# Causal attention with a gated MLP: the eighth pair of heads transposed by VectorE, and a new order of the steps

## The chip, the cores and the metric

The kernel runs on one core of a Trainium2 chip. The metric is the device time of one execution in microseconds (us), the median of several runs; lower is better.

## The reference

The input is q, k and v of 4 batches, 12 heads, 448 positions and 64 values per head. Causal attention gives x of 448 x 768 in every batch, and a gated MLP follows. Its second half v of the hidden values is normalised, mixed along the sequence by w_sg, and multiplies the first half u:

```python
scores = scale * np.matmul(q, k.transpose(0, 1, 3, 2))
scores = np.where(mask, -1000000000.0, scores)
attn = np.exp(scores - np.max(scores, axis=-1, keepdims=True))
attn = attn / (np.sum(attn, axis=-1, keepdims=True) + 1e-09)
x = np.matmul(attn, v)                       # heads side by side: 448 x 768
h = gelu(x @ w_in)                           # tanh form, 768 -> 1024
u, v = h[..., :512], h[..., 512:]
v_s = np.einsum('ts,bsd->btd', w_sg, layernorm(v) * g_ln) + b_sg[None, :, None]
out = x + (u * v_s) @ w_out                  # 512 -> 768
```

## The kernel before

**Attention.** The heads are worked on in pairs: 24 pairs, numbered from 0, six in each batch, so that the eighth pair has number 7 and is the second of the second batch. For one pair, `pair(p)` records these steps.

- SyncE (SP) loads q and k (line 424).
- TensorE (PE) computes the scores into four PSUM banks, in two steps (line 431). There are eight banks in all.
- VectorE (DVE) adds the mask and takes the maxima, eight instructions with the tile `ngm` (line 446).
- ScalarE (ACT) takes ten exponentials into P, with their sums (line 454).
- VectorE inverts the sums (lines 464 to 466), and two small transfers spread them over the partitions as `rb` (lines 471 and 474).
- P is transposed into B, in one of two ways (below).
- TensorE multiplies B by v in four steps (line 522), VectorE scales the result by `rb` (line 549), and GpSimd (POOL) and ScalarE split it into two parts (lines 555 to 560).

**Two ways to transpose P.** `flip = p >= FLIP` chooses. Without it, TensorE transposes P in four steps of four 128x128 blocks (line 496) into the banks tx and ty, and four copies bring these to B, by ScalarE (line 503) or, for one of the four in the first batch, by VectorE (line 501). With it, VectorE transposes P in two instructions of 1024 columns (line 484) into another P buffer, and four transfers on SP's queue bring this to B (line 488); v lies in another order in DRAM for such a pair. Before, FLIP is 8: pairs 0 to 7 go through TensorE, pairs 8 to 23 through VectorE.

**MLP.** `mlp(b)` needs x of all six pairs of a batch. It records the steps v (by token blocks 0 to 3, tile m, line 577), u (four), s (four) and o (six). All matmuls of the MLP have line 577. Each float32 operand is split into two parts, and three matmuls stand for one product. A step of a group holds three matmuls (`CUT = 3`). The last token block of v has 64 rows: its normalised values go to the tile `vn` in line 636 on VectorE, and every s needs it. The weights w_in, w_out and w_sg are split on the chip during the first batch (lines 350 to 374): VectorE shifts them (368, 370), ScalarE rescales (366), GpSimd casts and subtracts (373, 374).

**The order.** Every step is recorded by `od.add` with an engine, a duration that only a planner outside this file used, and the tiles it reads and writes. The steps are then issued in the order of the table `ORDER`, written out by hand or by that planner; the durations have no other effect on the program. All engines take their instructions in this order, each its own. A step that finds its inputs not ready holds up everything behind it on its engine. SP's queue works the same way: a transfer that waits holds up those behind it.

**The head of the program.** Seven dummy matmuls `warm` (steps 5 to 11, line 339) and one dummy exponential (step 3, line 330) are recorded. In the table before, the dummy matmuls stand behind the transposes of pairs 0 and 1, and the dummy exponential stands at place 1003 of 1883, so that the first exponential that ScalarE meets is one of pair 0 (step 96).

Of the kernel before, what the change touches and what calls it, by code (L numbers as in the profile page):

```python
# [12 lines left out]
AF = mybir.ActivationFunctionType  # L13
# [37 lines left out]
FLIP = 8  # L51
# [174 lines left out]
def attention_gated_mlp(ctx: ExitStack, tc: tile.TileContext, qk, vP, w_in, g_ln, w_sgT, b_sg, w_out, out):  # L226
# [100 lines left out]
    od.add("dve", 0.75, consts2, w=["P0", "sm0"])  # L327
    od.add("pool", 2.4, consts3, w=["P", "sm", ("wsg", "pad")])

    od.add("act", 0.2, lambda: nc.scalar.activation(out=pad[:, 0:1], in_=mhalf, func=AF.Exp), ["sm0"], ["table"])  # L330

    def warm():
        w = wz.t.bitcast(BF16)
# [432 lines left out]
```

## Time and profile before

| what | value |
|---|---|
| median of 3 runs | 339.13 us (338.38 to 340.37) |
| the profiled execution's own time | 337.29 us |
| its span | 335.5 us |
| TensorE busy | 324.1 us, 97% of the span |
| VectorE busy | 251.0 us, 75% |
| ScalarE busy | 208.5 us, 62% |
| GpSimd busy | 175.9 us, 52% |

Busy times are unions of an engine's instructions. An engine that is busy for 75% of the span can be the limit of a part of it, so shares are read by stretches. The chain that ended last goes back from the last instruction, at each step to what released it.

### The profile page before, as it was taken

How to read it: one execution, taken by the hardware profiler on the slowest of the kernel's cores; microseconds unless marked ns; L12 is line 12 of the kernel's file. 1: busy time of each engine (PE TensorE's matmuls, PEld its weight loads, DVE VectorE, ACT ScalarE, POOL GpSimd, SP SyncE). 2: the span in 40 equal slices, each digit the busy share in tenths (PEclk: the TensorE clock that was granted, in tenths of full speed). 3: DMA queues.
4: the chain of work that ended last, by engine and by line, in shares of the span. 5: the costliest groups of instructions: out<-in, count | busy, mean ns of one | idle time of the engine just before them, and what ended most of it. 6: DMA issues, size and time to landing. Idle time of an engine off the chain costs nothing.

```text
span 335.5 us, 7568 instructions
## 1 busy us (share of the span) xinstructions
PE 324.1 (97%) x2590; PEld 266.3 (79%) x2591; DVE 251.0 (75%) x762; ACT 208.5 (62%) x674; POOL 175.9 (52%) x225
## 2 busy tenths in 40 slices
PE   5699999999999999999999999999999999999995
PEld 3467678768887987878888978878989987889994
DVE  4899898999999888967977597889788531644613
ACT  1999999999894637666784526486674302355210
POOL 4258766888986964020535942014256824132691
PEclk9899999999999999999999999999999999999999
DMA  7889968595583688638747858739437440010004
GB/s 227 312 247 307 277 218 267 177 288 160 130 265 103 178 215 235 197 98 226 217 127 214 229 150 204 195 95 243 101 104 206 91 159 3 0 55 2 18 36 164
DMA packets 30965, 56.55 MB, mean 169 GB/s; under 512 B 6096, under 2 KB 15056, under 8 KB 30928
## 3 DMA queue, kind: packets, MB, share of 16 engines
q1 hardware_dynamic: 30928, 56.08, 57.5%
q8 instruction: 20, 0.33, 0.4%
q14 instruction: 17, 0.14, 0.1%
HBM read 33.39 MB, written 5.90 MB: 117 GB/s over the span
## 4 chain that ended last, share of the span: by engine, by line
PE 93%; ACT 4%; DMA 1%; DVE 1%; issue 0%; ACTq 0%; DVEq 0%
PE m L577 65%; PE o L522 13%; PE s L431 11%; ACT P L454 3%; PE ty L496 2%; PE tx L496 2%; DMA qk<-in_qk_dram 1%; PE m L339 0%; ACT L454 0%; ACT vn L366 0%; ACT B L503 0%; DVE s L446 0%; DVE res L702 0%; DVE ngm L446 0%; ACTq L454 0%
## 5 line engine op out<-in xcount | busy, mean ns | idle before, releaser
L454 ACT ACTIVATE P<-s,ngm 128x320 f32<-128x320 f32 (+3 forms) x240 | 102.7, 460 | 28.1 <-DVE ngm L446 19.7
L446 DVE CUSTOM_DVE_ANT_0 s<-s,mask 64x64 f32<-64x64 f32 (+3 forms) x192 | 77.6, 435 | 7.5 <-PE s L431 5.8
L577 PE MATMUL m<-win,x 128*128 128x512 f32 (+1 forms) x264 | 65.9, 399 | 0.0
L577 PE MATMUL m<-g,wout 128*128 128x448 f32 x288 | 61.1, 367 | 0.0
L577 PE MATMUL m<-x,win 128*128 128x448 f32 x288 | 61.1, 367 | 0.0
L577 PEld LDWEIGHTS m<-x,win 128*128 128x128 f32 x288 | 53.9, 188 | 5.0
L577 PEld LDWEIGHTS m<-g,wout 128*128 128x128 f32 x288 | 53.9, 188 | 5.0
L577 PEld LDWEIGHTS m<-win,x 128*128 128x128 f32 (+1 forms) x264 | 47.4, 183 | 11.7
L454 ACT ACTIVATION_READ_ACCUMULATOR P<-s,ngm 128x1 f32 (+1 forms) x240 | 55.1, 233 | 0.0
L431 PE MATMUL s<-qk 64*64 64x64 f32 (+5 forms) x768 | 45.2, 371 | 5.0 <-DMA qk<-in_qk_dram 4.4
L431 PEld LDWEIGHTS s<-qk 64*64 64x64 f32 x768 | 30.7, 139 | 21.6 <-issue 8.5
L522 PE MATMUL o<-B,vraw 128*64 128x64 f32 (+4 forms) x672 | 45.0, 291 | 0.0
L522 PEld LDWEIGHTS o<-B,vraw 128*64 128x64 f32 x672 | 32.8, 137 | 12.7 <-issue 4.5
L484 DVE STREAM_TRANSPOSE P<-P 128x1024 f32<-128x1024 f32 x32 | 38.2, 1224 | 0.7 <-DMA B<-P 0.6
L577 PE MATMUL m<-wsg,vn 128*128 128x448 f32 x176 | 38.3, 369 | 0.0
L621 POOL TENSOR_TENSOR mv<-mv,mhalf 128x1 f32<-128x1 f32 (+1 forms) x16 | 10.0, 626 | 49.0 <-DVE mv L619 40.7
L577 PEld LDWEIGHTS m<-wsg,vn 128*128 128x128 f32 x176 | 32.6, 188 | 3.6 <-DVE vn L636 0.4
L558 POOL TENSOR_TENSOR x<-xt,x 128x448 fp32r<-128x448 f32 x24 | 27.5, 1148 | 14.5 <-ACT x L557 14.2
L702 DVE TENSOR_TENSOR res<-m,res 128x448 f32<-128x448 f32 (+1 forms) x25 | 14.8, 603 | 23.2 <-PE m L577 15.2
L586 DVE SCALAR_TENSOR_TENSOR tmp<-tmp,m 128x448 f32<-128x448 f32 (+1 forms) x28 | 17.9, 640 | 16.2 <-ACT tmp L585 16.0
L673 POOL TENSOR_TENSOR tmp<-tmp,g 128x448 f32<-128x448 f32 x16 | 18.3, 1152 | 18.8 <-DVE tmp L669 18.8
L585 ACT ACTIVATE tmp<-m 128x448 f32<-128x448 f32 (+1 forms) x28 | 15.5, 562 | 20.3 <-PE m L577 19.2
(76 smaller groups left out, 410.8 us busy)
## 6 DMA issues: line engine op xcount, KB each, us to landing
B<-P SPq DMA_DIRECT2D x64, 256.0 KB
qk<-in_qk_dram SPq DMA_DIRECT2D x24, 448.0 KB
vn<-in_w_in_dram SPq DMA_DIRECT2D x12, 512.0 KB
vraw<-in_vP_dram SPq DMA_DIRECT2D x24, 256.0 KB
rb<-rd SPq DMA_DIRECT2D x24, 224.0 KB
out_dram<-res SPq DMA_DIRECT2D x9, 448.0 KB
g<-in_w_out_dram SPq DMA_DIRECT2D x16, 192.0 KB
out_dram<-res SPq DMA_DIRECT2D x5, 224.0 KB
```

The costliest lines, as they stand in the source:

```text
L431: nc.tensor.matmul(out=s[z][bk].t[64 * h:64 * h + 64, col:col + n], lhsT=qk_.t[r, 0, q0:q0 + 64], rhs=qk_.t[r, 1, k0:k0 + n], start=True, ...
L446: nc.vector.tensor_tensor_reduce(out=o, in0=i, in1=mk, scale=-0.125, scalar=3e38, op0=ALU.add, op1=ALU.min, accum_out=ngm[ib[z]][c][0:m])
L454: act(n, lambda c=c, m=m, k0=k0, n=n, bk=bk, col=col, off=off, kc=kc, i=i, z=z: nc.scalar.activation(out=P[i][0:m, off:off + n], in_=s[z][ ...
L484: dve(PW, lambda z=z: nc.vector.transpose(A[ia][:, :, :, z, :].rearrange("p g t k -> p t g k"), P[ib[z]]), Pk[z] + [kp], Ak, 1.105)
L496: nc.tensor.transpose(out, P[ib[z]][:, col:col + 128], ident)
L522: nc.tensor.matmul(out=dst(o.t[r]), lhsT=vr.t[:, c, r], rhs=src(z), start=first and n == 0, stop=last and n == len(lst) - 1)
L558: pool_tt(S, lambda: nc.gpsimd.tensor_tensor(out=y.t[:, S + 64:], in0=x.t, in1=f(y.t)[:, 0:S], op=ALU.subtract), [x, y], [(y, 1)])
L577: nc.tensor.matmul(out=ps.t[0:l().shape[1], 0:n], lhsT=l(), rhs=rr(), start=(k == 0), stop=(k == len(mms) - 1))
L585: act(n, lambda: nc.scalar.activation(out=z(), in_=h(), func=AF.Square), [ps], [t])
L586: dve(n, lambda: nc.vector.scalar_tensor_tensor(out=z(), in0=z(), scalar=1.0 / GC, in1=h(), op0=ALU.add, op1=ALU.mult), [ps], [t])
L673: pool_tt(S, lambda z=z, u=u: nc.gpsimd.tensor_tensor(out=z(), in0=z(), in1=u.t, op=ALU.mult), [u], [t])
L702: dve(hi - lo, lambda rr=rr, ps=ps, z=z, lo=lo, hi=hi: nc.vector.tensor_tensor(out=rr.t[:, z, lo:hi], in0=ps.t[:, lo:hi], in1=rr.t[:, z, l ...
```

## The change

- `FLIP` goes from 8 to 7. Pair 7 has its P transposed by VectorE (two instructions of line 484) and moved by four transfers (line 488). Its four TensorE steps of transposes and their four copies by ScalarE go. TensorE has 522 steps in place of 526, ScalarE 428 for 432, VectorE 515 for 513, SP 212 for 208.
- The exponentials read the key "table" that the dummy exponential writes, so a table has to place that one ahead of them. Both are on ScalarE; no wait is added.
- Durations used by the planner are set anew, and some steps are marked as sharing a port (`port`). This has no effect on the program but through the table.
- `ORDER` is new from end to end.

What the two tables say, as far as the prediction speaks of it:

- The dummy exponential is fourth in the new table. Three dummy matmuls stand ahead of the first scores and four between the scores of pair 1 and the second transpose of pair 0.
- VectorE's step of line 636 in batch 0 (the last token block of v). Ahead of it on VectorE stand, in the new table but not in the old, the two transposes of pair 7, the first transpose of pair 10, the scaling of pair 8 (line 549), one shift of line 368 and one of line 370 of w_out. In the old table but not in the new there stand two steps of line 586 (u) and the halving of two constants (lines 395 and 396).
- TensorE's first step that reads the result of that line 636 (an s step). Ahead of it on TensorE stand, in the new table but not in the old, the four steps of pair 8's multiplication by v. In the old table but not in the new there stand the four transposes of pair 7 and one s step of three matmuls.
- By the time that VectorE has taken the maxima of pair 6, 13 steps of line 368 have gone ahead of them in the new table, and 9 in the old.
- The multiplications by v of pairs 6 and 7 stand next to each other in both tables. The two transposes of pair 7 stand on VectorE ahead of the maxima of pair 9.
- The last TensorE step is one of o's last block in the new table (its result is added in two halves and leaves in two transfers of 112 KB) and one of o's fourth block in the old (one addition, one transfer of 224 KB).

```diff
-FLIP = 8
+FLIP = 7
...
-    84, 85, 86, 1, 4, 0, 2, 89, 87, 90, 96, 88, 95, 98, 91, 92, 97, 99, 93, 94, 125, 126, 128, 127, 12, 18, 13, 103,
...
+    2, 1, 0, 3, 4, 5, 6, 7, 84, 85, 87, 125, 89, 88, 95, 90, 96, 86, 93, 91, 94, 92, 97, 12, 98, 126, 127, 8, 100, 13,
...
-    od.add("act", 0.2, lambda: nc.scalar.activation(out=pad[:, 0:1], in_=mhalf, func=AF.Exp), ["sm0"], ["table"])
+    od.add("act", 1.35, lambda: nc.scalar.activation(out=pad[:, 0:1], in_=mhalf, func=AF.Exp), ["sm0"], ["table"])
...
-                    [s[z][bk], ("ngm", i, c), kp, ks] + ([("P", i, k - 1)] if k == 1 else [("P", i, 2)] if k == 4 else []),
+                    [s[z][bk], ("ngm", i, c), kp, ks, "table"] + ([("P", i, k - 1)] if k == 1 else [("P", i, 2)] if k == 4 else []),
...
-        od.add("dve", 0.42, inv, sk + [ks], [("rT", ip)])
+        od.add("dve", 0.573, inv, sk + [ks], [("rT", ip)])
...
-    def gelu2(ps, m, n, dst=None):
+    def gelu2(ps, m, n, dst=None, port=False):
```

## Rows read from the trace of the kernel before

**Rows 1.** The page, parts 1 and 4: busy time, and the last chain by engine.
```profile
PE 324.1 (97%) x2590; PEld 266.3 (79%) x2591; DVE 251.0 (75%) x762; ACT 208.5 (62%) x674; POOL 175.9 (52%) x225
...
PE 93%; ACT 4%; DMA 1%; DVE 1%; issue 0%; ACTq 0%; DVEq 0%
```
**Rows 2.** The chain that ended last in order of time: start, duration, what.
```profile
3.92 1.88 PE s L431 x8
...
7.07 1.28 ACT L454
...
19.46 0.49 ACT B L503
...
21.40 1.24 PE m L339 x5
...
64.73 0.44 PE tx L496 x4
...
126.64 3.68 PE o L522 x64
...
276.38 55.46 PE m L577 x263
```
**Rows 3.** Stretches: length, busy of PE, PEld, DVE, ACT, POOL, clock, DMA share, GB/s.
```profile
5.94:98.46 92.52, 88.67 (x822) 67.60 (x815) 86.50 (x321) 88.12 (x310) 64.98 (x80) 0.98 0.78 242
...
20.00:60.00 40.00, 39.95 (x417) 28.97 (x419) 37.13 (x146) 39.95 (x151) 27.92 (x33) 1.00 0.85 265
60.00:98.46 38.46, 38.46 (x299) 30.81 (x297) 37.10 (x126) 35.26 (x113) 33.18 (x43) 1.00 0.68 200
```
**Rows 4.** VectorE's timeline from 92 to 104 us: start, duration, line, operation.
```profile
93.87 0.15 DVE L395 TENSOR_SCALAR gcol<-gcol 128x4 f32<-128x4 f32 x1
93.94 0.37 DVE L396 TENSOR_SCALAR bB<-bB 128x448 f32<-128x448 f32 x1
...
96.03 1.13 DVE L586 SCALAR_TENSOR_TENSOR tmp<-tmp,m 128x448 f32<-128x448 f32 x2
...
97.77 0.69 DVE L636 TENSOR_TENSOR vn<-tmp,vn 64x512 fp32r<-64x512 f32 x1
```
**Rows 5.** TensorE's weight loads: what they waited for, total us, times, longest.
```profile
PEld m L577 <- DVE vn L636: 0.4, 2, 0.2
```
**Rows 6.** Groups by line with shapes apart, whole run: busy us, mean ns, idle before.
```profile
L484 DVE STREAM_TRANSPOSE P<-P 128x1024 f32<-128x1024 f32 x32 | 38.2, 1224 | 0.7 <-DMA B<-P 0.6
...
L549 DVE TENSOR_TENSOR xt<-o,rb 128x448 f32<-128x448 f32 x24 | 14.6, 615 | 7.7 <-PE o L522 4.0 <-DMA rb<-rd 2.1 <-POOL x L555 0.7
...
L503 ACT ACTIVATE B<-tx 128x512 f32<-128x512 f32 x16 | 10.0, 703 | 0.0
```
**Rows 7.** Stretches of 1 and of 5 us, columns as in rows 3.
```profile
15.00:16.00 1.00, 1.00 (x17) 0.99 (x11) 0.96 (x5) 1.00 (x7) 0.00 (x0) 0.50 0.15 57
...
65.00:70.00 5.00, 5.00 (x46) 4.03 (x48) 5.00 (x17) 4.97 (x21) 4.40 (x10) 1.00 0.99 262
```
**Rows 8.** Timeline: VectorE's first maximum, ScalarE's first exponential.
```profile
5.94 0.23 DVE L446 CUSTOM_DVE_ANT_0 s<-s,mask 64x64 f32<-64x64 f32 x1 [3.88 <-PE s L431]
...
8.37 0.63 ACT L454 ACTIVATE P<-s,ngm 128x448 f32<-128x448 f32 x1
```
**Rows 9.** TensorE's first scores from 4.6 us, and the same later, from 23 us.
```profile
L431 PE MATMUL s<-qk 64*64 64x448 f32 x4 | 1.8, 978 | 3.9 <-DMA qk<-in_qk_dram 3.9
...
L431 PE MATMUL s<-qk 64*64 64x448 f32 x4 | 1.0, 562 | 0.0
```
**Rows 10.** TensorE's timeline from 92 to 104 us: the s steps.
```profile
94.88 6.18 PE L577 MATMUL m<-wsg,vn 128*128 128x448 f32 x28
```
**Rows 11.** VectorE's groups from 60.00 to 98.46 us: the shifts of w_out.
```profile
L370 DVE SCALAR_TENSOR_TENSOR g<-g 128x192 int32<-128x192 int32 x10 | 3.1, 342 | 0.0
L368 DVE TENSOR_SCALAR g<-g 128x192 int32<-128x192 int32 x9 | 2.9, 337 | 0.0
```
**Rows 12.** VectorE's longest wait from 60.00 to 98.46 us: total, times, longest.
```profile
DVE tmp L586 <- ACT tmp L585: 0.7, 1, 0.7
```

More of the change, by code (lines that the diff above doesn't have):

```diff
@@ L474, in pair @@
         dma(lambda: nc.sync.dma_start(out=rb.t, in_=bass.AP(
-            tensor=rd[ip].tensor, offset=rd[ip].offset, ap=[[512, 8], [0, 16], [1, S]])), [("rd", ip)], [rb], 320e3, dur=0.56)
+            tensor=rd[ip].tensor, offset=rd[ip].offset, ap=[[512, 8], [0, 16], [1, S]])), [("rd", ip)], [rb], 360e3, dur=0.56)
         Pk = [[("P", i, c) for c in range(5)] for i in ib]
@@ L586, in gelu2 @@
         dve(n, lambda: nc.vector.scalar_tensor_tensor(out=z(), in0=z(), scalar=1.0 / GC, in1=h(), op0=ALU.add,
-                                                      op1=ALU.mult), [ps], [t])
+                                                      op1=ALU.mult), [ps], [t], port=port)
         act(n, lambda: nc.scalar.activation(out=z(), in_=z(), func=AF.Tanh, scale=GS * GC), [], [t], True)
@@ L590, in gelu2 @@
         dve(n, lambda: nc.vector.scalar_tensor_tensor(out=z() if dst is None else d.t, in0=z(), scalar=1.0, in1=h(),
-                                                      op0=ALU.add, op1=ALU.mult), [ps, t], [d])
+                                                      op0=ALU.add, op1=ALU.mult), [ps, t], [d], port=port)
         return t, z
@@ L614, in mlp @@
                                                                      op=ALU.add), [ps], [hs])
-                t, z = gelu2(hs, m, DH)
+                t, z = gelu2(hs, m, DH, port=True)
             st, mv = buf(two, "st", [128, 6]), buf(two, "mv", [128, 3])
@@ L622, in mlp @@
                 out=mv.t[0:m, 1:2], in0=mv.t[0:m, 1:2], in1=mhalf[0:m], op=ALU.pow), ["sm0"], [mv])
-            od.add("dve", 0.07, lambda mv=mv, m=m: nc.vector.tensor_scalar(
+            od.add("dve", 0.125, lambda mv=mv, m=m: nc.vector.tensor_scalar(
                 out=mv.t[0:m, 2:3], in0=mv.t[0:m, 0:1], scalar1=mv.t[0:m, 1:2], scalar2=-1.0, op0=ALU.mult, op1=ALU.mult),
@@ L626, in mlp @@
             act(DH, lambda mv=mv, z=z, m=m: nc.scalar.activation(
-                out=z(), in_=z(), func=AF.Identity, scale=mv.t[0:m, 1:2], bias=mv.t[0:m, 2:3]), [mv], [t], True)
+                out=z(), in_=z(), func=AF.Identity, scale=mv.t[0:m, 1:2], bias=mv.t[0:m, 2:3]), [mv], [t], True, 2)
             if m == 128:
@@ L636, in mlp @@
                 dve(DH, lambda y=y, z=z: nc.vector.tensor_tensor(out=y.t[64:128], in0=z(), in1=f(y.t)[0:64],
-                                                                 op=ALU.subtract), [t, y], [(y, 1)])
+                                                                 op=ALU.subtract), [t, y], [(y, 1)], port=True)
             vn[tcn] = y
```

178 rows, old and new, of the table ORDER are left out of this document.

## The prediction

> **What bounds the kernel now.** I began with the page. TensorE is busy for 97% of the span and the last chain is 93% TensorE [rows 1], so the first reading is "bound by TensorE". The chain in order of time says when this is true. ScalarE carries it from 7.07 us, where a load of its function table stands (1.28 us), to the copy that ends at 19.95; from there TensorE carries it without a break worth naming to 276.38 + 55.46 = 331.84 [rows 2]. So there are two lengths to look at: a head in which TensorE waits for ScalarE, and some 312 us in which every microsecond of TensorE counts.
>
> The view by stretches adds what the chain cannot show, who stands close behind. From 20 to 60 us ScalarE is busy 39.95 of 40 us. VectorE is busy 37.13 of 40 there and 37.10 of 38.46 from 60 to 98.46 us [rows 3]. Neither has room there; after the first batch both have. The change takes work from TensorE and ScalarE and gives VectorE more, in just these stretches. The point at which this is decided can be seen: line 636 on VectorE, the last input of the mixing along the sequence, ends at 97.77 + 0.69 = 98.46 us [rows 4], and TensorE waited there, twice for 0.2 us [rows 5]. VectorE and TensorE arrive there together today.
>
> **The change, part by part.**
>
> *TensorE loses the transposes of pair 7:* four steps of 0.44 = 1.76 us, all on the chain, of which the first at 64.73 stands in [rows 2] and the others at 67.26, 67.69 and 68.13 are alike. The multiplication by v takes 3.68 us for two pairs that come through VectorE, or 1.84 for one [rows 2]; the columns multiplied are the same, so I count nothing for it beyond 0.03. Net -1.73 us.
>
> *ScalarE loses four copies,* 4 x 0.70 = 2.8 us at most [rows 6], beside other work. They are worth something only where ScalarE is last.
>
> *VectorE gets two transposes,* 2 x 1.22 = 2.45 us [rows 6]. Behind them in its queue stand the maxima of pair 9, and behind those the exponentials.
>
> *SP gets four transfers* of 256 KB in its queue; the first of them waits for VectorE's transposes, with loads of weights behind it. The DMA engines moved 262 GB/s at a share of 0.99 between 65 and 70 us [rows 7], so 1 MB is some 4 us of them (an estimate from that row). I take nothing: pair 7 is multiplied next to pair 6, as before, several microseconds after its transposes. If that cover fails, the multiplication is late by up to those 4 us; the low end is zero, since nothing becomes earlier.
>
> *The table load moves out of the head.* It ends at 7.07 + 1.28 = 8.35 [rows 2], and the first exponential starts at 8.37 [rows 8]. With the dummy exponential fourth, the load runs while ScalarE has no inputs, and the exponentials start 1.28 us earlier.
>
> *The seven dummy matmuls leave the chain,* where they take about 1.5 us (1.24 for the last five [rows 2]). In the new table they stand where TensorE waits. But ScalarE is full until 60 us, and TensorE cannot run ahead of the copies and exponentials it needs; so I count ScalarE's 1.28 us as TensorE's lead and not the sum of 2.8. Both ends stay for a rival.
>
> *TensorE's clock in the head.* The first 64x448 score matmuls took 978 ns, later ones 562 [rows 9]: the first step ran slowly, and dummies ahead of it may change that by up to 0.9 us, half of the 1.88 that the chain has for it [rows 2]. They may also be too few. Later in the head the granted clock was 0.50, the 1.2 GHz level, between 15 and 16 us [rows 7]; the chain is on ScalarE there, so it cost nothing. I take zero of 0 to 0.9.
>
> *The order.* What counts is what stands ahead of the meeting point at line 636.
>
> For TensorE: out go pair 7's transposes (1.76) and one s step, three matmuls of 6.18/28 = 0.22 [rows 10], 0.66; in comes pair 8's multiplication, 1.84. That is -0.58, and -1.28 for the head: its own arrival goes from 98.46 to 96.6. Behind the point, 331.84 - 98.46 = 233.38 us remain today, and -1.73 + 0.58 = -1.15 of the saving falls here: 232.23.
>
> For VectorE: in come three transposes (3 x 1.22 = 3.67), a scaling (0.61) [rows 6] and two shifts (0.34 + 0.34) [rows 11]; out go two steps of line 586 (1.13) and the halving (0.15 + 0.37) [rows 4]. That is 4.96 - 1.65 = +3.3 us. Against this stands its idle time: from 5.94 us, its first maximum [rows 8], to 98.46 it was busy 86.50 of 92.52, so 6.0 idle [rows 3]. About 1.1 of this are gaps between instructions that stay (from 60 to 98 us it was idle for 1.36 beside 37.10 of work, and 0.9 of this were waits, the longest 0.7 [rows 12]; the other 0.46 make 1.2% of the work); 4.9 were waits. The new table has 13 shifts in place of 9 ahead of pair 6's last maxima, so more work is at hand where VectorE waited. I let it win back 3.5 of the 4.9: an in-order queue always keeps some waits, and from 60 us on, with work at hand, it still had those 0.9. Ends: 0 and 4.9.
>
> **The sum.** VectorE's line 636 ends at 98.46 + 3.3 - 3.5 = 98.26, later than TensorE's 96.6; so it decides, and most of TensorE's lead from the head is lost in waiting here. 98.26 + 232.23 = 330.49 in place of 331.84, **-1.35 us**. The tail (now a smaller last transfer) I leave unchanged. The profiled execution would go from 337.29 to 335.9; it lay 1.84 under the median of the runs shown, so against that median, 339.13 - 1.35 = **337.8 us**, -0.4%. What a measurement of this kernel can tell from no change is about 0.5%, 1.7 us: my forecast lies inside.
>
> **The rivals.**
>
> *A. VectorE fills all its waits* (4.9 us). Then line 636 ends at 96.86 and the gain is 98.46 - 96.86 + 1.15 = 2.75: 336.4 us. If the dummies also speed up the first scores, VectorE starts up to 0.9 earlier and TensorE's own arrival goes with it: 3.65, 335.5. For it: the head, where ScalarE starts earlier, and the shifts moved forward. Against it: in-order waits never vanish. With TensorE alone as the limit (the 1.5 us of the dummies too) it would be 4.6, but VectorE cannot be so early.
>
> *B. Slower: VectorE becomes the limit.* It meets as many waits as before on its new path, wins nothing back, and line 636 ends at 98.46 + 3.3 = 101.8; TensorE stands still there for 3.3 us more and ends at 334.0, +2.15: 341.3 us. The tip-over lies at 2.15 us won back. For it: VectorE is at 93 to 96% already, and the transposes of pair 7 push the maxima of pair 9 back. Against it: its waits today are waits for others that will be earlier. The Trainium skill ("VectorE: DVE Perf Modes", Rules for kernel authors) says to transpose 128x128 on TensorE where PSUM will do as destination. By that rule this change goes the wrong way, and rival B is its price here; [rows 2, 6] show that VectorE's 2.45 us for a pair are more than TensorE's 1.76, so the change can pay only where VectorE has idle time.
>
> *C. Nothing to be seen for another reason:* the transfers of pair 7 are late, TensorE waits up to 4 us at its multiplication, and that wait takes the place of the one at line 636: 337.8 to 339.5.
>
> **How the numbers follow.** My forecast, with 2.1 to 4.4 us won back, has 0.55: of this 0.40 lies within 0.5%, and 0.15 (over 3.8 won back) is faster by more. A has 0.27, nearly all of it faster. B has 0.13. C has 0.05, within. Together: faster 0.42, same 0.45, slower 0.13. The range reaches into A down to 335.2, just below its lower price, and into B up to 340.3, where VectorE wins back 1 us; what is left out is B's upper half and luck beyond A, under 2 in 10.
>
> **What would show it.** Right: the table load ahead of 5 us and the first exponential at its maximum's end, near 7.1; no dummy matmul on the chain; transposes of line 496 for 28 steps, not 32; VectorE over 96% busy from 20 to 98 us; and a wait of TensorE for VectorE of 1 to 2 us near line 636 of the first batch, where now it is 0.2. Wrong: if TensorE waits for nothing there and the gain is over 3 us, VectorE had more to win back than I gave it (A). If TensorE waits there for 3 us or more, B. If the wait is at a multiplication by v near 70 to 75 us, C. If ScalarE's first exponential is not earlier, the head was misread.

## The result: 0.7% slower, and VectorE's shifts grew by eight to ten microseconds

The median after is 341.11 us (339.61 to 343.52, 13 runs) against 338.75 (337.71 to 340.37, 13 runs) on the same chip: ratio 1.0073, 95% interval 1.0045 to 1.0100. That is 2.4 us slower, above the range of the prediction. The profiled execution took 343.52 us, the longest of the 13; a second one of the same kernel (below, a_again) has a span of 339.0 in place of 341.7 us, and where the two differ, both are given.

**The page after**, the lines that answer to [rows 1]:

```profile
PE 326.2 (95%) x2587; PEld 264.4 (77%) x2587; DVE 261.1 (76%) x764; ACT 206.9 (61%) x670; POOL 175.2 (51%) x225
...
PE 74%; DVE 15%; DMA 5%; issue 2%; ACT 1%; POOL 1%; DVEq 0%; SPq 0%
```

VectorE holds 15% of the last chain where it held 1% (13% in the second execution), and its busy time grew by 10 us (7.7 in the second), although it got only two instructions more.

**Stretches after**, with the columns of [rows 3]; the first runs from VectorE's first maximum to the end of its line 636, as 5.94 to 98.46 us did before:

```profile
6.02:106.17 100.15, 90.68 (x845) 65.95 (x837) 97.37 (x323) 85.93 (x311) 65.09 (x82) 1.00 0.78 237
20.00:60.00 40.00, 37.22 (x393) 26.24 (x394) 37.57 (x142) 37.64 (x147) 27.28 (x33) 1.00 0.83 258
60.00:98.46 38.46, 34.44 (x259) 26.41 (x258) 38.28 (x94) 28.17 (x91) 27.42 (x35) 1.00 0.72 205
```

From 60 to 98.46 us VectorE is busy for 38.28 of 38.46, and with 94 instructions; before there were 126 in 37.10 us [rows 3]. An engine that does fewer instructions in more time does longer ones, or its instructions have become longer. Groups by line with shapes apart tell which. **The shifts of the weights up to 98.46 us, before:**

```profile
L370 DVE SCALAR_TENSOR_TENSOR vn<-vn 128x512 int32<-128x512 int32 x12 | 8.3, 690 | 0.6 <-ACT vn L366 0.5
L370 DVE SCALAR_TENSOR_TENSOR g<-g 128x192 int32<-128x192 int32 x14 | 5.5, 414 | 0.0
L368 DVE TENSOR_SCALAR vn<-vn 128x512 int32<-128x512 int32 x12 | 5.1, 425 | 0.1
L368 DVE TENSOR_SCALAR g<-g 128x192 int32<-128x192 int32 x15 | 4.4, 319 | 0.0
```

**and after:**

```profile
L370 DVE SCALAR_TENSOR_TENSOR vn<-vn 128x512 int32<-128x512 int32 x12 | 9.4, 783 | 0.4 <-ACT vn L366 0.4
L370 DVE SCALAR_TENSOR_TENSOR g<-g 128x192 int32<-128x192 int32 x11 | 8.9, 813 | 0.0
L368 DVE TENSOR_SCALAR g<-g 128x192 int32<-128x192 int32 x15 | 7.4, 500 | 0.0
L368 DVE TENSOR_SCALAR vn<-vn 128x512 int32<-128x512 int32 x12 | 7.0, 584 | 0.0
```

The same work on the same shapes: 32.7 us for 50 instructions after, 23.3 for 53 before. At the mean lengths of before the 50 would take 12 x 0.690 + 11 x 0.414 + 15 x 0.319 + 12 x 0.425 = 22.7 us, so the shifts are **10.0 us longer** (by the same sum 8.2 in the second execution). Nearly all else of VectorE kept its length (line 484 has 1225 ns on the page after, 1224 in [rows 6]; an exception is line 636 itself, 0.95 us for 0.69).

What a long shift stands beside is in the timelines. **VectorE after:**

```profile
66.10 2.36 DVE L370 SCALAR_TENSOR_TENSOR g<-g 128x192 int32<-128x192 int32 x1
68.38 0.84 DVE L370 SCALAR_TENSOR_TENSOR vn<-vn 128x512 int32<-128x512 int32 x1
69.14 2.15 DVE L370 SCALAR_TENSOR_TENSOR g<-g 128x192 int32<-128x192 int32 x2
...
105.22 0.95 DVE L636 TENSOR_TENSOR vn<-tmp,vn 64x512 fp32r<-64x512 f32 x1
```

**and GpSimd after:**

```profile
65.38 1.16 POOL L353 TENSOR_TENSOR wsg<-tmp,wsg 64x448 fp32r<-64x448 f32 x1 [2.01 <-ACT wsg L352]
66.50 0.63 POOL L373 CAST win<-vn 128x512 fp32r<-128x512 f32 x1
67.09 1.15 POOL L353 TENSOR_TENSOR wsg<-tmp,wsg 128x448 fp32r<-128x448 f32 x1
68.19 0.47 POOL L373 CAST wout<-g 128x192 fp32r<-128x192 f32 x1
68.75 0.94 POOL L374 TENSOR_TENSOR wout<-g,wout 128x192 fp32r<-128x192 f32 x1
69.65 1.43 POOL L374 TENSOR_TENSOR win<-vn,win 128x512 fp32r<-128x512 f32 x1
```

The shift at 66.10 is in flight for 2.36 us while GpSimd runs three instructions back to back, and it ends soon after the third. Beside no GpSimd instruction such a shift takes 0.34 us in both traces, one of w_in 0.69; those of line 368 take 0.25 and 0.42. Counted in the traces up to the end of line 636 (overlaps of more than 0.02 us), 28 of 53 shifts stood beside no GpSimd instruction before, 18 beside nothing but casts or line 621 (which works on one column), and 7 beside one of GpSimd's wider instructions with two inputs (lines 353, 374, 558 and others). After, it is 19, 7 and 29 of 55. In both orders the first two kinds keep those lengths to within 0.2 us. The 29 grew by 12.3 us together, 22 of them by more than 0.1 us each (10.5 us and 20 in the second execution); the 7 of before grew by 1.7 us.

**TensorE after: what it waited for up to 110 us** (total, times, longest), and the end of the chain:

```profile
PE s L431 <- DVE tmp L590: 2.7, 2, 1.6
PE m L339 <- DVE tmp L334: 2.1, 1, 2.1
PE s L431 <- DVE B L501: 1.4, 2, 1.2
PE ty L496 <- ACT P L454: 1.3, 3, 0.8
PE m L577 <- DVE tmp L590: 1.1, 1, 1.1
PE tx L496 <- ACT P L454: 1.1, 1, 1.1
...
```
```profile
282.63 55.56 PE m L577 x263
```

The wait of line 339 is that of the dummy matmuls, ahead of the first scores. Behind it TensorE stands still for VectorE at several places ahead of line 636, for 2.7 + 1.4 + 1.1 = 5.2 us in these rows (1.6 + 1.4 + 0.5 = 3.5 in the second execution). That line ends at 105.22 + 0.95 = 106.17 us, and TensorE at 282.63 + 55.56 = 338.19, which is 232.0 us later.

**The head after**, ScalarE's timeline:

```profile
0.73 1.28 ACT L330 ACT_TABLE_LOAD   x1 [0.73 <-PEq L755]
...
7.17 0.63 ACT L454 ACTIVATE P<-s,ngm 128x448 f32<-128x448 f32 x1 [4.94 <-DVE ngm L446]
```

The table load has left the head, and the first exponential starts at 7.17 in place of 8.37 us [rows 8]. The first scores take 1.93 us on the chain, as before (1.88 in [rows 2]).

### The profile page after: what moved, and what is told of

The parts are those of the page before. It is cut to its first block, busy times and chain, and to the rows that moved or that the text cites. A ratio compares the mean times of both kernels' runs of the same rounds, so it can differ in the third digit from the quotient of the medians.

```text
span 341.7 us, 7550 instructions
## 1 busy us (share of the span) xinstructions
PE 326.2 (95%) x2587; PEld 264.4 (77%) x2587; DVE 261.1 (76%) x764; ACT 206.9 (61%) x670; POOL 175.2 (51%) x225
## 4 chain that ended last, share of the span: by engine, by line
PE 74%; DVE 15%; DMA 5%; issue 2%; ACT 1%; POOL 1%; DVEq 0%; SPq 0%
PE m L577 58%; PE o L522 9%; PE s L431 7%; DVE s L446 5%; DMA rb<-rd 2%; DVE g L370 2%; DVE g L368 1%; DVE P L484 1%; ACT P L454 1%; DVE ngm L446 1%; DMA vn<-in_w_in_dram 1%; DMA rd<-rT 1%; DMA qk<-in_qk_dram 1%; DVE vn L368 1%; DVE vn L370 1%
## 5 line engine op out<-in xcount | busy, mean ns | idle before, releaser
L454 ACT ACTIVATE P<-s,ngm 64x64 f32<-64x64 f32 (+3 forms) x240 | 100.6, 434 | 31.4 <-DVE ngm L446 27.8
L446 DVE CUSTOM_DVE_ANT_0 s<-s,mask 64x64 f32<-64x64 f32 (+3 forms) x192 | 76.6, 436 | 6.7 <-PE s L431 6.0
L577 PE MATMUL m<-win,x 128*128 128x512 f32 (+1 forms) x264 | 65.0, 398 | 1.5 <-DVE tmp L590 1.1
L577 PE MATMUL m<-x,win 128*128 128x448 f32 x288 | 62.2, 368 | 0.2 <-DVE xt L549 0.2
L431 PE MATMUL s<-qk 64*64 64x64 f32 (+5 forms) x768 | 47.2, 364 | 5.4 <-DVE tmp L590 2.7
L454 ACT ACTIVATION_READ_ACCUMULATOR P<-s,ngm 128x1 f32 (+1 forms) x240 | 49.8, 208 | 0.0
L484 DVE STREAM_TRANSPOSE P<-P 128x1024 f32<-128x1024 f32 x34 | 41.1, 1225 | 3.1 <-ACT P L454 2.4
L522 PEld LDWEIGHTS o<-B,vraw 128*64 128x64 f32 x684 | 33.6, 137 | 12.6 <-issue 4.1
L577 PEld LDWEIGHTS m<-wsg,vn 128*128 128x128 f32 x176 | 32.7, 188 | 3.2 <-DVE vn L636 0.4
L689 POOL TENSOR_TENSOR res<-x 128x448 f32<-128x448 f32 x24 | 27.3, 1152 | 7.4 <-DMA out_dram<-res 5.5
L588 ACT ACTIVATE tmp<-tmp 128x448 f32<-128x448 f32 (+2 forms) x32 | 19.1, 602 | 18.1 <-DVE tmp L586 17.9
```

What stands on the lines that cost most here:

```text
L431: nc.tensor.matmul(out=s[z][bk].t[64 * h:64 * h + 64, col:col + n], lhsT=qk_.t[r, 0, q0:q0 + 64], rhs=qk_.t[r, 1, k0:k0 + n], start=True, ...
L446: nc.vector.tensor_tensor_reduce(out=o, in0=i, in1=mk, scale=-0.125, scalar=3e38, op0=ALU.add, op1=ALU.min, accum_out=ngm[ib[z]][c][0:m])
L454: act(n, lambda c=c, m=m, k0=k0, n=n, bk=bk, col=col, off=off, kc=kc, i=i, z=z: nc.scalar.activation(out=P[i][0:m, off:off + n], in_=s[z][ ...
L484: dve(PW, lambda z=z: nc.vector.transpose(A[ia][:, :, :, z, :].rearrange("p g t k -> p t g k"), P[ib[z]]), Pk[z] + [kp], Ak, 1.105)
L522: nc.tensor.matmul(out=dst(o.t[r]), lhsT=vr.t[:, c, r], rhs=src(z), start=first and n == 0, stop=last and n == len(lst) - 1)
L577: nc.tensor.matmul(out=ps.t[0:l().shape[1], 0:n], lhsT=l(), rhs=rr(), start=(k == 0), stop=(k == len(mms) - 1))
```

## Theories and experiments

**Theory S:** the new order puts VectorE's shifts beside GpSimd's splits of the weights; there they are held up, and VectorE becomes the limit up to some 95 us. **Its rivals:** the way that pair 7 now takes costs the time (F), or the new order costs it by waits that have nothing to do with the shifts' length (O). In the short diffs below, numbers are steps of the table `ORDER`; those of a_ kernels are steps of the new table, those of b_ kernels of the old. Each time is a median, with runs of the kernel before on the same chip beside it; the ratios are to these, and times of different chips are best compared by them.

**a_again.** The kernel after, unchanged.

> The changed kernel once more, for a second profile. In the first profile the four groups of VectorE's shifts (lines 368 and 370) took 35.3 us together, against 24.6 before, with the same 56 instructions. Theory S (VectorE's shifts are held up by GpSimd's splits wherever the new table puts the two side by side): 30 us or more again, time 341 +- 1 us. Theory F (the two transposes of pair 7, 2.45 us, are the whole loss, and the long shifts were an accident of one execution): 24 to 28 us, with the time still 341.

341.08 us, ratio 1.0074 [1.0045, 1.0103]. The shifts take 33.5 us over the whole run (24.6 in the kernel before), and line 636 ends at 102.49 + 0.96 = 103.45 us. The loss and the long shifts stand in both executions.

**a_noflip.** The new table, pair 7 through TensorE.

```diff
-FLIP = 7
+FLIP = 8
 ORDER: steps 688, 689 (two transposes) -> 688 to 691 (TensorE's four), 692 to 695 (the copies)
```

> The new table with pair 7 back on TensorE: its four transposes and copies stand where VectorE's two transposes stood. Theory F: the loss goes, 338.8 us or less. Theory S / O: the loss stays, 340 to 343 us, and the shifts take 30 us or more.

343.89 us, ratio 1.0146 [1.0104, 1.0188]; shifts 34.9 us. The time is a little above the range of S and O. Taking the flip back makes the kernel 2.8 us slower than a_again, so F falls: in the new table the flip is a gain, and the loss lies in the table.

**b_flip.** The old table with the flip, the transposes right behind pair 7's last exponential, the transfers behind its small transfer of line 471.

```diff
-FLIP = 8
+FLIP = 7
 ORDER: ... last exponential of pair 7, +688, +689 ... 686, +690, +691, +692, +693 ...
```

> The old table with pair 7 transposed by VectorE: its two transposes stand behind the last exponential of pair 7, its four transfers behind the small transfer of its sums; nothing else moves. Theory F: VectorE is full, so the kernel loses about what the new one lost, 340 to 341.5 us. Theory S / O (it is the new table that loses): TensorE's 1.73 us against VectorE's 2.45 nearly cancel, 337.5 to 339.5 us, and the shifts take 24 to 28 us.

344.82 us, ratio 1.0180 [1.0138, 1.0222], with shifts of 25.0 us: slower than either range that was expected. So the old table loses by the flip, and for another reason than the new one. SP's queue, when each transfer was issued and for how long:

```profile
66.62 0.57 SPq L471 DMA_DIRECT2D rd<-rT  x1
67.28 3.32 SPq L488 DMA_DIRECT2D B<-P  x4
70.65 1.34 SPq L474 DMA_DIRECT2D rb<-rd  x1
```

The reciprocals come behind the two transposes, and the broadcasts and the weights behind the four transfers: the row of line 474 that stood at 62.59 us in the trace before now starts at 70.65. (Some 2.4 of these 8 us were lost before 57 us, where VectorE's line 464 already stood at 56.83 in place of 54.38.)

**b_flip2.** The same, with the transposes behind the reciprocals, and the transfers behind the broadcasts and a load of w_in (steps 646, 687 and 72, which stand further forward in the table).

```diff
 ORDER: ... 685, 686, +688, +689 ... 646, 72, 687, +690, +691, +692, +693, first transpose of pair 8 ...
```

> The old order with pair 7 through VectorE, as in b_flip, but VectorE's two transposes behind the row of reciprocals of pair 7 (line 466) in place of ahead of it, and SP's four transfers behind the two broadcasts (line 474) and the load of w_in in place of ahead of them. Theory F (b_flip lost by SP's queue: it stood still for the transposes with the broadcasts and weights behind it): most of the 6 us goes, 338 to 341 us. If the flip costs the old order because VectorE has no room for 2.45 us more before 98 us: 341 to 344 us, with VectorE over 98% busy from 60 to 98 us.

342.79 us, ratio 1.0130 [1.0093, 1.0166]. A good quarter of b_flip's loss goes, not most of it; where the rest comes from stays open. Its profiled execution was 4 us longer than its median, so the rows tell the place and not the size of the loss. TensorE's longest wait, and VectorE at that time:

```profile
PE o L522 <- DMA vn<-in_w_in_dram: 4.0, 1, 4.0
```
```profile
78.10 1.25 DVE L484 STREAM_TRANSPOSE P<-P 128x1024 f32<-128x1024 f32 x1 [3.12 <-DMA B<-P]
```

The multiplication by v waits 4.0 us for a transfer; the row names a load of w_in, which lies just ahead of pair 7's four transfers in the queue, and VectorE waits for those four by name. This would be the price that rival C had for late transfers, in the old table; but the wait is as long as what this execution took above the median, and b_flip's profile has none like it, so it isn't shown for the usual execution. VectorE was busy for 33.97 of 38.46 us from 60 us on, so the mechanism of the expectation's other branch is not what happened, although the time falls into it.

**a_memset and b_memset.** In both kernels line 374 writes zeros; the low halves of w_in and w_out are left out.

```diff
-pool_tt(n, lambda: nc.gpsimd.tensor_tensor(out=dst(1), in0=f(lo()), in1=f(dst(0)), op=ALU.subtract),
+pool_tt(n, lambda: nc.gpsimd.memset(f(dst(1)), 0.0),
```

> The kernel after, with line 374 (GpSimd's subtraction that makes the low halves of w_in and w_out) replaced by a GpSimd memset of the same 512 or 192 columns to zero; it leaves out the low halves of these weights. GpSimd then reads nothing from SBUF there and is done sooner; the columns that TensorE multiplies are the same. Theory S (VectorE's shifts of lines 368 and 370 are held up by GpSimd's split working beside them): the shifts fall from 33.5 to 35.3 us to at most 28, VectorE's load from 60 to 98 us falls below 37, and the time falls by 3 us or more against the kernel after, to 338 or less. Theory O (the new order loses by waits that have nothing to do with the shifts' lengths): the shifts may fall, but the time stays within 1 us of 341.

> The kernel before with the same memset in place of line 374 (the low halves of w_in and w_out left out), as the baseline for the same edit in the kernel after. Theory S: its shifts were hardly held up (24.6 us), so they stay at 22 to 25 us and the time stays within 1 us of 338.8; the two kernels with the memset differ by less than 1 us. Theory O: the same here, but the kernel after with the memset stays 2 us or more above this one.

After: 338.06 us, ratio 0.9997 [0.9968, 1.0026], 3.0 us under a_again (2.6 by the ratios). Before: 339.70, ratio 1.0034 [1.0012, 1.0055], 1.4 us over its own kernel, a little more than expected; its shifts took 26.3 us, above the 22 to 25 that were expected, and what else it lost by was not followed. With GpSimd's subtraction out of both, the kernel after is 1.6 us faster than the kernel before, where O wanted it 2 us slower and S the two within 1 us. The shifts of the kernel after with the memset, up to 98.46 us:

```profile
L370 DVE SCALAR_TENSOR_TENSOR vn<-vn 128x512 int32<-128x512 int32 x12 | 9.9, 826 | 0.3 <-ACT vn L366 0.3
L368 DVE TENSOR_SCALAR vn<-vn 128x512 int32<-128x512 int32 x12 | 7.1, 589 | 0.0
L370 DVE SCALAR_TENSOR_TENSOR g<-g 128x192 int32<-128x192 int32 x15 | 6.4, 429 | 0.0
L368 DVE TENSOR_SCALAR g<-g 128x192 int32<-128x192 int32 x16 | 5.2, 333 | 0.0
```

Those of w_out fell from means of 813 and 500 ns to 429 and 333; those of w_in stayed long (826, 589); GpSimd's other subtractions (lines 353 and 558) still run beside some of them. The sum of 28.6 us missed the expected 28, and VectorE's load from 60 to 98.46 us, 38.04 us, did not fall below 37. In this kernel GpSimd is also done sooner, so this run alone doesn't say whether the lengths or GpSimd's earlier end gave the time; the next one does.

**a_apart.** The kernel after with every instruction kept; the nine rows with the longest shifts (ten instructions) are moved to where GpSimd was idle.

```diff
 ORDER (step L368 or L370 -> its new place)
 376, 50 -> ahead of 382;  353 -> ahead of 44;  371, 359, 401 -> behind 62;  365, 377 -> ahead of 68
 69 -> behind 68;  418 -> ahead of 424;  GpSimd's 366, 367, 378, 379 -> ahead of 384
```

> The kernel after with the same instructions; in its order table nine of VectorE's shifts (lines 368 and 370, those that ran longest over their length at rest beside a GpSimd instruction) are moved to places where GpSimd stood idle in the trace of the kernel after, and four of GpSimd's splits (lines 373, 374) go behind two of them. Theory S (shifts are held up by GpSimd's instructions): these nine ran some 8.5 us over their length; half or more of it goes, the shifts up to 98 us fall from 33.5 to 35.3 us to below 30, VectorE's line 636 of batch 0 ends 2 us or more earlier than at 105.2, and the time falls by 2 to 4 us against the kernel after, to 337 to 339. Theory O (the new order loses by other waits): 340.5 to 342, whatever the shifts do.

337.65 us, ratio 0.9976 [0.9952, 1.0000], **3.4 us faster than the kernel after** (3.3 by the ratios) from a move of 14 of 1881 steps. The shifts up to 98.46 us take 28.4 us for 55 instructions, and line 636 ends at 99.20 + 0.96 = 100.16 us, 3.3 to 6.0 us earlier than in the two executions of the kernel after. The stretch from VectorE's first maximum to that end, which holds as many of VectorE's instructions (323) as in the kernel after:

```profile
6.03:100.16 94.13, 89.31 (x845) 65.57 (x837) 91.59 (x323) 85.74 (x311) 64.05 (x82) 1.00 0.82 254
```

VectorE is busy there for 91.59 us, against 97.37 and 95.60 in the two executions of the kernel after, and idle for 94.13 - 91.59 = 2.54, against 2.78 and 1.80. So line 636 is earlier because VectorE's instructions are shorter, and not because of other waits. Theory S holds, O falls.

**a_apart2.** Seven more shifts moved.

```diff
 ORDER: 412, 418, 424, 406, 407, 395, 80 -> ahead of 81 (behind line 613)
```

> The kernel with the shifts moved apart (a_apart) once more: six shifts of w_out and one of w_in, which still ran some 2.8 us over their length between 81 and 88 us, go behind line 613, where GpSimd stood idle from 88.1 to 89.6 us. Theory S: their stretching goes as before (the shifts up to 98 us fall from 28.3 to 26 us or less). The time can fall by no more than TensorE still stands idle for VectorE, so 336.4 to 337.6. If VectorE no longer limits there: no change, 337.7.

337.80 us, ratio 0.9974 [0.9960, 0.9989]. The shifts (up to 98.46 us), the stretches from 60 us and from the first maximum to the end of line 636, and VectorE's longest wait for ScalarE:

```profile
L370 DVE SCALAR_TENSOR_TENSOR vn<-vn 128x512 int32<-128x512 int32 x12 | 8.4, 699 | 0.7 <-ACT vn L366 0.5
L368 DVE TENSOR_SCALAR vn<-vn 128x512 int32<-128x512 int32 x12 | 6.0, 503 | 0.0
L370 DVE SCALAR_TENSOR_TENSOR g<-g 128x192 int32<-128x192 int32 x15 | 5.2, 365 | 0.0
L368 DVE TENSOR_SCALAR g<-g 128x192 int32<-128x192 int32 x16 | 4.1, 270 | 0.0
```
```profile
6.08:100.68 94.60, 89.81 (x845) 65.85 (x837) 87.67 (x323) 85.49 (x311) 64.12 (x82) 1.00 0.81 251
60.00:98.46 38.46, 37.04 (x272) 28.87 (x271) 33.78 (x111) 30.97 (x101) 29.04 (x42) 1.00 0.75 225
```
```profile
DVE tmp L613 <- ACT tmp L611: 3.4, 1, 3.4
```

23.7 us for 55 shifts, as short as in the old table, and the time doesn't move: with 33.78 us in 38.46 VectorE is no longer the limit. It waits 3.4 us at line 613 for ScalarE's line 611, which ends at 87.39 us, as in a_apart (87.35), so line 636 ends no earlier (100.68 us). Of the two branches that were expected it is the second.

**b_table, b_dummy, b_head.** The old table with the new head in parts: the dummy exponential alone, the dummy matmuls alone, both.

```diff
 b_table: step 3 -> ahead of 0
 b_dummy: 1, 4, 5, 6, 7 -> ahead of 85;  8, 9, 10, 11 -> ahead of 127
 b_head:  1, 3, 4, 5, 6, 7 -> ahead of 85;  8, 9, 10, 11 -> ahead of 127
```

> The kernel before with the dummy exponential alone moved to the front (the table load out of the head); the dummy matmuls stay where they were. If the 1.6 us that b_head won are ScalarE's 1.28 us handed through to TensorE: 337.2 to 337.8. If they come from the dummy matmuls (1.5 us off TensorE's chain): 338.3 to 338.8.

> The kernel before with the dummy matmuls alone moved as in b_head (three more ahead of the first scores, four ahead of pair 1's second step of scores); the load of the function table stays in the head. If b_head's 1.6 us come from the matmuls alone: 336.8 to 337.4. If the matmuls and the load are worth something only together, since each alone leaves the other engine as the limit of the head: 338 to 339.

> The old table with the head of the new one alone: the dummy exponential second on ScalarE's side ahead of all others, three dummy matmuls ahead of the first scores, four between the two score steps of pair 1. If ScalarE's 1.28 us reach the end: 337.5 us (-1.3). If VectorE at line 636 (98.5 us) takes it back: 338.7 us, with a longer wait of TensorE there. If the dummies too are gained: 336 us. First exponential at 7.1 us in any case.

b_table: 338.56 us, 1.0003 [0.9981, 1.0025]. b_dummy: 337.97, 0.9987 [0.9963, 1.0011]. b_head: 337.18, 0.9955 [0.9925, 0.9985]. Either part alone can't be told from nothing; together they gave 1.6 us in the median. The intervals of the three overlap, so that the two parts are worth more together than alone isn't shown. In the profiled executions they differ in the granted clock (the third number from the end). Stretches of 1 us from 14 us on, first b_table:

```profile
14.00:15.00 1.00, 1.00 (x18) 0.86 (x12) 1.00 (x4) 1.00 (x7) 0.00 (x0) 0.50 0.72 265
15.00:16.00 1.00, 1.00 (x8) 1.00 (x6) 0.94 (x5) 1.00 (x5) 0.80 (x2) 0.50 0.69 168
```

then b_dummy:

```profile
14.00:15.00 1.00, 0.85 (x7) 0.84 (x11) 0.80 (x5) 1.00 (x6) 0.10 (x1) 0.50 0.80 305
15.00:16.00 1.00, 1.00 (x19) 0.98 (x11) 0.97 (x5) 1.00 (x7) 0.00 (x0) 0.50 0.36 131
```

then b_head:

```profile
14.00:15.00 1.00, 0.95 (x20) 0.65 (x10) 0.97 (x4) 1.00 (x7) 0.00 (x0) 1.00 0.70 270
15.00:16.00 1.00, 0.64 (x4) 0.40 (x4) 0.96 (x6) 1.00 (x5) 0.70 (x2) 1.00 0.48 130
```

In these executions TensorE falls to 0.50, the 1.2 GHz level, around 15 us with one part alone and is busy nearly all the time; with both it stays at 1.00 and has time to spare. What in its earlier work makes the difference these rows don't settle: from 12 to 13 us it was busy for 0.69 us in b_table and 0.58 in b_head, both at 1.00. Nor does the clock explain the times. Of b_table's 12 executions 7 have a granted clock of 0.998 or more over the whole span, and their median is 339.07 us, against 337.79 for the other 5. In b_head it is 7 at 336.61 us and 5 at 337.99, in b_head2 7 at 337.96 and 5 at 337.51. Of the 98 executions of the kernel before that ran beside these experiments, 8 have 0.998 or more, with a median of 338.5 us, and the other 90 have 338.7.

**b_head2.** b_head again, beside a_apart2.

> The kernel with the new head alone (b_head, unchanged) on the same chip as the one with the shifts moved apart, to see which is the better of the two: 337.2 as before.

337.66 us, ratio 0.9980 [0.9959, 1.0002]. The two runs of b_head give 1.2 and 1.6 us in the median; the interval of this one just reaches 1. Between it and the kernels with the shifts apart no difference can be told. All of them lie 0.2 to 0.5% under the kernel before, of which only b_head's first run and a_apart2 are wholly clear of it, and some 3 us or more under the kernel after.

## Why the prediction was wrong

**The step that failed is the sum for VectorE, "+3.3 us", in which two shifts came in at "0.34 + 0.34" and all others at the length that they had.** Up to the end of line 636 VectorE worked 97.37 us where it had worked 86.50 [rows 3]: +10.9 us (95.60 in the second execution, +9.1). The groups of its shifts take 34.6 us there for 55 (32.8 in the second execution), where they took 23.3 for 53: 11.3 us more (9.5), of which the sum had 0.68. (An engine's instructions overlap a little at their ends, so the groups add up to somewhat more than its busy time.) I took their length from [rows 11]. There 16 of the 19 stand beside a GpSimd instruction, but all of these beside casts or line 621 and only one of them beside a subtraction too, and I carried this into an order in which 29 of 55 stand beside GpSimd's wider instructions with two inputs. The old trace had the warning: a shift of line 370 took 1.31 us at 58.20, beside a subtraction of line 353 that ran from 57.65 for 1.65 us. I looked at the mean of a stretch that begins at 60.00 us, 342 ns, and this one lies just ahead of it.

**What VectorE wins back came out near in size, and that is luck.** It had 6.0 us of idle time, I let it win back 3.5, and it has 100.15 - 97.37 = 2.78 left, so it won back 3.2 (in the second execution 1.80 are left, 4.2 won back). But that more work at hand fills its waits isn't shown: in a_apart2, with the shifts back at their old length, VectorE idles for 94.60 - 87.67 = 6.93 us, and wins back nothing. That waits shrink on an engine that is itself late would fit both. Nor is it a proof of the sum that a_apart2's 337.80 us meets the forecast of 337.8: there VectorE's work grew by 1.2 us and not by 3.3. And "busy" on an engine that is held up in the middle of an instruction is no work: "VectorE over 96% busy" came true ((37.57 + 38.28) / 78.46 = 97%) for the wrong reason.

**The meeting point.** Line 636 should have ended at 98.26 and ended at 106.17, in the second execution at 103.45. From there I gave TensorE 232.23 us; it took 232.0 in both. So the parts of the sum that belong to TensorE (pair 7's transposes, pair 8's multiplication moved) stood to 0.2 us, and the whole error lies ahead of this point. The wait of 1 to 2 us "near line 636" didn't come: there it is 0.4 us, and TensorE's waits for VectorE stand earlier, at scores and at v.

**Rival B** gave 341.3 us, and 341.11 was measured. It was right in that VectorE becomes the limit; its price is not what happened, so the agreement is luck: it let VectorE win nothing back for +3.3 us of work, and there were 3.2 to 4.2 us less of idle time for +9.1 to +10.9 us of work. The rule of the Trainium skill that stood beside B ("VectorE: DVE Perf Modes", Rules for kernel authors: transposes on TensorE) is not borne out in the new table: with pair 7 back on TensorE the kernel is 2.8 us slower (a_noflip). In the old table it is: there the way through VectorE costs 4.5 to 6.0 us (b_flip2, b_flip).

**Rival C** is not seen in the kernel after, where none of TensorE's listed waits up to 110 us is for a transfer of pair 7. "I take nothing" for SP's four transfers held. In the old table one execution of b_flip2 shows such a wait (4.0 us), with the reserve given there.

**The head** came as foretold in its times (7.17 for 7.1 us, no dummy matmul on the chain). Zero for the first scores held (1.93 us for 1.88, with three dummy matmuls ahead). The clock I counted as costing nothing, since "the chain is on ScalarE there"; the executions of b_table and of the kernel before that kept it were not faster, so no cost of it is shown. The sum for the head, 1.28 us of TensorE's lead, lies between the medians of the two runs of b_head (1.2 and 1.6), whose intervals are wider than that.

**Why the mechanism could have been known.** That shifts become long beside GpSimd is shown by the two moves (a_apart, a_apart2), which change nothing but the order. The Trainium skill names a cause ("SBUF — State Buffer", Who interferes with whom): a VectorE instruction with two SBUF inputs contends with a GpSimd instruction that reads SBUF, but not with one that only writes it, and one of the two waits for the other. This agrees with line 370, whose shifts have two inputs: in a_memset one kept its 0.68 us beside a memset (from 29.12 us), which took its usual 0.51, and the shifts of w_out fell. It says nothing of line 368, whose shifts have one input and made 5.7 of the 12.3 us (5.7 of 10.5 in the second execution); in b_memset one of them took 1.36 us at 87.36, beside a cast and memsets. In these traces the loss went with the number of meetings with GpSimd's wider two-input instructions, 7 and 29 by the count above; I did not look for them in the old trace.

## What to carry to other kernels

A duration read from a trace belongs to its neighbours too. Before a step is costed at its mean, look at the longest of its group, over the whole run, and at what the other engines did just then; where there is a long one, a new order must be costed by how often it brings the two together. And an edit that gains in one order can lose in another (the flip: 2.8 us gained in the new table, 4.5 to 6.0 lost in the old), so test it in the order that it comes with.

## What was not expected of the hardware

- A VectorE instruction in flight was overtaken by several of GpSimd's. The shift at 66.10 us was in flight when GpSimd's cast at 66.50 and its subtraction at 67.09 began, and it ended only at 68.46. The page cited above says that whichever issues first gets what the two share, for the whole instruction. By that the shift should have come ahead of the cast; in this row, as far as GpSimd's spans can be trusted, it did not.
- The other side pays too: line 374 on w_in, 1428 ns in the mean after, took 2.05 us at 29.29 us, where a shift of w_in ran beside it at its usual 0.68. Between a shift and a cast it was mostly the cast that grew. Before, the casts of w_out took 0.35 us in the mean beside no shift and 0.69 beside one; the longest stood beside three shifts that kept their lengths:

```profile
80.00 1.19 POOL L373 CAST wout<-g 128x192 fp32r<-128x192 f32 x1 [1.13 <-DVE g L370]
```

- The granted clock of 0.50 in the head [rows 7] is not seen in the time. The kernel before kept 0.998 or more over the span in 8 of 98 executions, with a median of 338.5 us, and took 338.7 in the others.
